# Plain blocks on TensorE, row sums in a column, one exp per head, and a new end: a change to a decode attention kernel that streams K and V

## The chip, the cores and the metric

The kernel runs on one core of a Trainium2 chip. The metric is the device time of one execution in microseconds (us). A ratio is the mean time of one kernel's fast runs over the mean of the other's fast runs of the same rounds, so it isn't quite the ratio of the medians that are quoted beside it.

## The reference

One query token attends to 65,536 keys. There are 32 query heads and 8 key heads, so 4 query heads share a key head, and the head dimension D is 128. Everything is bfloat16.

```python
B, Hq, Hkv, Sq, Sk, D = 1, 32, 8, 1, 65536, 128
scores = jnp.einsum("bhqd,bhkd->bhqk", q, k) * D ** -0.5
p = jax.nn.softmax(scores, axis=-1)
return jnp.einsum("bhqk,bhkd->bhqd", p, v)
```

K and V are 134.2 MB each. Every byte is used once.

## The kernel before

For each key head (G = 8) the K rows come in two loads of 8.39 MB (128 partitions x 256 slots x 128 elements), and so do the V rows. K has two buffers, V has one that is refilled in place. VectorE transposes K, TensorE computes scores, VectorE finds the maximum, ScalarE takes exp, VectorE transposes the weights, and TensorE multiplies them with V one head later. SyncE issues all loads, each as soon as the buffer is free:

```python
def load_k(g, b):
    SP.wait((s_sc, 16 * g - 8 + 8 * b if g else 0))     # scores of the head before are done
    ...
def load_v(g, b):
    done = 2 * (2 * g + b)
    if (g, b) == (G - 1, 1):                            # the last one comes in pieces
        ...
        for lo, hi, s in list(zip(CUTS, CUTS[1:], s_v))[1:]:
            load(v, g, b, 0, s, lo, hi)
    ...
    else:
        SP.wait((s_vc, done))                           # the V before has been multiplied
        load(v, g, b, 0, s_v[0])
        for s in s_v[1:4]:
            sp.sem_inc(s, 16)                           # credits for semaphores this load doesn't use
```

The softmax and TensorE's loop, cut:

```python
for b in range(4):
    a = act.activation(out=ex[:, b, :], in_=sc[:, 512 * b:512 * b + 512], func=ACT.Exp,
                       bias=nmb[:, :], scale=SCALE, accum_out=ls[:, b:b + 1])
...
with nc.Fori(0, G + 1, 1, engines=OrderedEngineSet([PE])) as h:
    ...
    gather(start=True, stop=True).then_inc(s_pe, 1)              # sums of the head before
    pe.matmul(out=pl, lhsT=sel[:, :], rhs=ls[:, :], ...)         # row sums of the head before
    with pe.Fori(0, 2) as j:
        with pe.If(h < G):
            with pe.Fori(0, 8) as n: ...                         # 8 score matmuls each
        with pe.If(h * 2 + j > 1):
            for ch in range(4):
                ...                                              # 16 matmuls with V each
                if ch == 1:
                    for _ in range(3):                           # fillers, result not used
                        pe.matmul(out=pt[0:16, :], lhsT=et[:, 0, 0:16], rhs=et[:, 0, :], ...)
```

After the loop come 24 small matmuls (128x4 by 128x128) for the last 24 slots of V, one at a time as the last pieces land, then a gather that adds up what was accumulated before, then the scale by 1/sum and the store:

```python
for x in range(TAIL):                                            # TAIL = 24
    if x % 8 == 0:
        pe.wait_ge(s_v[4 + x // 8], 16)
    pe.matmul(out=fin, lhsT=et[:, 1, w0:w0 + H], rhs=io[:, t, :], ...)
pe.wait_ge(s_vs, 1)
gather(start=False, stop=True).then_inc(s_pe, 1)
```

## Time and profile before

| | before |
|---|---|
| median of 3 runs | 631.59 us (631.14 to 631.75) |
| span of the profiled run | 629.3 us |
| bytes on the load queue | 268.44 MB |
| busy: TensorE, VectorE, ScalarE | 57%, 55%, 6% |
| one 8.39 MB load to the next, in the middle | 19.35 us, so 433.5 GB/s |
| last byte has landed | 625.32 us |

The first view is the page of the kernel before: busy time of each engine, then rows by slice (40 equal slices of the span, tenths; PEclk is TensorE's granted clock), then the DMA queues with packets, MB and share, and the exps of ScalarE with busy time and mean ns of one.

```profile
PE 355.6 (57%) x2176; PEld 141.5 (22%) x2176; DVE 347.1 (55%) x239; ACT 36.7 (6%) x72; POOL 7.4 (1%) x39
...
PEclk9999695976959789597896968869698696999568
DMA  8999999999999999999999999999999999999996
...
q1 hardware_dynamic: 6488, 268.44, 98.9%
...
q14 instruction: 4, 0.03, 0.0%
q8 instruction: 1, 0.02, 0.0%
...
L262 ACT ACTIVATE ex<-sc,nmb 128x512 bf16<-128x512 f32 x32 | 21.6, 686 | 556.1 <-DVE nmb L259 556.1
...
L262 ACT ACTIVATION_READ_ACCUMULATOR ex<-sc,nmb 128x1 f32 x32 | 6.5, 203 | 0.0
```

The DMA row is the one that is full, and the load queue keeps the DMA engines busy for 98.9% of the span. TensorE is idle for 43% of the span. Five small transfers on two queues are of the kind "instruction". I take them for fetches of code: with 128 more waits in VectorE's stream (dvewaits, below) three were recorded, at 13.8, 260.4 and 571.3 us, in place of the changed kernel's two.

The timeline of SyncE's queue in the middle shows when loads are issued (start us, us, what):

```profile
93.86 0.33 SPq L125 DMA_DIRECT2D io<-in_v_dram  x1
...
131.97 0.33 SPq L125 DMA_DIRECT2D io<-in_v_dram  x1
```

The landing of the transfer ahead of these V loads, from the records of landings: 101.67 us for the one issued at 93.86, and 140.38 us for the one issued at 131.97. In the middle a V load is always queued 8 to 9 us before the load ahead of it has landed on all 16 DMA engines. That is the slack of everything that computes.

The chain of waits, in order of time (start us, us, what; cut), shows the end:

```profile
610.52 13.57 DMA io<-in_v_dram
624.10 0.57 issue
624.66 1.50 PE pf L431 x24
626.16 0.23 PE pf L355 x2
...
```

A load is waited for, and then come small matmuls, gather, scale, store and the closing of the program: 4.0 us from the last landing (625.32) to the end of the span (629.30) in which no load moves.

### The profile page before, as it was taken

The numbers are of one execution on the slowest core, as the hardware profiler recorded it, in microseconds if no ns is written. First come the engines' busy times: TensorE is split into PE (matmuls) and PEld (weight loads), VectorE is DVE, ScalarE is ACT, GpSimd is POOL, SyncE is SP. The second block draws the span as 40 slices with busy tenths as digits, with TensorE's granted clock in tenths as the row PEclk, the third lists the DMA queues.
The fourth block names the chain that finished last, engine by engine and source line by source line (L and its number), as shares of the span: only waits on it lengthen the run. The fifth ranks groups of instructions, "written<-read, shape, count | busy, mean of one in ns | idle before, by whom it ended". The sixth has DMA issues, their size and how long they took to land. (4 is left out here: it accounts for less than half of the span.)

```text
span 629.3 us, 7142 instructions
## 1 busy us (share of the span) xinstructions
PE 355.6 (57%) x2176; PEld 141.5 (22%) x2176; DVE 347.1 (55%) x239; ACT 36.7 (6%) x72; POOL 7.4 (1%) x39
## 2 busy tenths in 40 slices
PE   0676581747627366382754728547184571886445
PEld 0222230312203122131321303213031230332112
DVE  4984925739066490665807557084670947684201
ACT  0000200020000200002000020000200002000100
POOL 1000000000000000000000000000000000000000
PEclk9999695976959789597896968869698696999568
DMA  8999999999999999999999999999999999999996
GB/s 367 433 459 408 458 408 455 412 454 412 454 412 454 417 450 417 450 417 450 421 446 421 446 425 442 425 442 425 446 425 442 429 437 429 409 433 431 431 428 247
DMA packets 6597, 268.50 MB, mean 427 GB/s; under 512 B 832, under 2 KB 832, under 8 KB 1344
## 3 DMA queue, kind: packets, MB, share of 16 engines
q1 hardware_dynamic: 6488, 268.44, 98.9%
q10 hardware_dynamic: 104, 0.02, 0.0%
q14 instruction: 4, 0.03, 0.0%
q8 instruction: 1, 0.02, 0.0%
HBM read 268.44 MB, written 0.01 MB: 427 GB/s over the span
## 5 line engine op out<-in xcount | busy, mean ns | idle before, releaser
L383 PE MATMUL sc<-io,wz 128*128 x1024 | 267.3, 411 | 201.5 <-PEq L345 158.4
L237 DVE STREAM_TRANSPOSE io<-io 128x4096 uint32<-128x4096 uint32 x64 | 279.8, 4417 | 162.8 <-DMA io<-in_k_dram 162.8
L383 PEld LDWEIGHTS sc<-io,wz 128*128 x1024 | 104.7, 102 | 361.0 <-issue 282.0
L359 PE MATMUL vacc<-io,et 128*16 128x512 bf16 x1018 | 73.5, 409 | 19.8 <-PEq L345 19.7
L262 ACT ACTIVATE ex<-sc,nmb 128x512 bf16<-128x512 f32 x32 | 21.6, 686 | 556.1 <-DVE nmb L259 556.1
L242 DVE TENSOR_REDUCE mx<-sc 128x1 f32<-128x512 f32 x32 | 20.8, 667 | 46.0 <-PE sc L383 46.0
L359 PEld LDWEIGHTS vacc<-io,et 128*16 128x16 bf16 x1018 | 27.7, 92 | 57.9 <-issue 35.8
L281 DVE STREAM_TRANSPOSE et<-ex 128x512 bf16<-128x512 bf16 x32 | 20.6, 683 | 15.4 <-PE vacc L359 13.5
L355 PE MATMUL pf<-vs,sel 128*4 128x128 f32 x20 | 5.4, 368 | 26.8 <-PEq L345 26.8
L251 DVE TENSOR_REDUCE m<-pt 1x4 f32<-1x128 f32 x8 | 2.2, 278 | 32.2 <-PE pt L419 32.2
L408 PE MATMUL pt<-et 128*16 128x512 bf16 x48 | 13.7, 397 | 0.0
L272 ACT ACTIVATE sc<-zero 128x2048 f32<-128x2048 f32 x7 | 13.2, 1880 | 0.3
L224 POOL COPY wz<-qT 32x16 bf16<-32x16 bf16 x32 | 6.1, 191 | 507.8 <-PE sc L383 502.5
L372 PE MATMUL pb<-ls,sel 128*4 128x4 f32 x18 | 1.8, 168 | 15.3 <-PEq L345 15.3
L290 DVE TENSOR_SCALAR vs<-vacc,sely 128x128 f32<-128x128 f32 x8 | 2.6, 324 | 13.3 <-PE vacc L359 13.3
L293 DVE SCALAR_TENSOR_TENSOR vs<-vacc,sely,vs 128x128 f32<-128x128 f32 x24 | 8.4, 351 | 0.8
L355 PEld LDWEIGHTS pf<-vs,sel 128*4 128x4 f32 x20 | 1.2, 83 | 27.2 <-issue 27.2
L262 ACT ACTIVATION_READ_ACCUMULATOR ex<-sc,nmb 128x1 f32 x32 | 6.5, 203 | 0.0
L421 PE MATMUL pb<-one,nrow 1*128 1x1 f32 x16 | 3.0, 254 | 5.7 <-PEq L345 5.7
L408 PEld LDWEIGHTS pt<-et 128*16 128x16 bf16 x48 | 4.6, 95 | 6.6 <-issue 1.6
L372 PEld LDWEIGHTS pb<-ls,sel 128*4 128x4 f32 x18 | 1.2, 88 | 18.9 <-issue 18.8
L421 PEld LDWEIGHTS pb<-one,nrow 1*128 1x128 f32 x16 | 2.5, 198 | 7.1 <-issue 7.1
(29 smaller groups left out, 25.5 us busy)
## 6 DMA issues: line engine op xcount, KB each, us to landing
io<-in_v_dram SPq DMA_DIRECT2D x5, 4096.0 KB, 15.7
io<-in_k_dram SPq DMA_DIRECT2D x4, 4096.0 KB, 26.0
io<-in_k_dram SPq DMA_DIRECT2D x4, 2048.0 KB, 38.8
io<-in_v_dram SPq DMA_DIRECT2D x1, 2048.0 KB, 11.1
io<-in_v_dram SPq DMA_DIRECT2D x1, 1024.0 KB, 13.3
io<-in_v_dram SPq DMA_DIRECT2D x4, 256.0 KB, 13.6
io<-in_k_dram SPq DMA_DIRECT2D x13, 46.6
io<-in_v_dram SPq DMA_DIRECT2D x13, 28.2
```

What stands on the lines that cost most here:

```text
L224: gp.tensor_copy(out=wz[r, :, c0:c0 + H].rearrange("p (s w) h -> p s w h", s=2), in_=qTb[r, :, :, g, :],).then_inc(s_w, 1)
L237: dve.transpose(out=part.bitcast(u32), in_=part.bitcast(u32)).then_inc(s_kt, 2)
L242: return DV.mark(dve.tensor_reduce(out=mx[:, b:b + 1], in_=sc[:, 512 * b:512 * b + 512], axis=AX.X, op=ALU.max))
L262: a = act.activation(out=ex[:, b, :], in_=sc[:, 512 * b:512 * b + 512], func=ACT.Exp, bias=nmb[:, :], scale=SCALE, accum_out=ls[:, b:b + 1],)
L272: ACTQ.mark(act.activation(out=sc[:, :], in_=zero[:, 0:1].to_broadcast([P, 4 * 512]), func=ACT.Copy))
L281: dve.transpose(out=et[:, i, :], in_=ex[:, 2 * b + i, :]).then_inc(s_et, 1)
L293: i = dve.scalar_tensor_tensor(out=vs[:, :], in0=vacc[:, y, :], scalar=sely[:, y:y + 1], in1=vs[:, :], op0=ALU.mult, op1=ALU.add,)
L355: return pe.matmul(out=fin, lhsT=sel[:, :], rhs=vs[:, :], skip_group_check=True, **kw)
L359: return pe.matmul(out=vacc[32 * c:32 * c + 16, :, :], lhsT=et[:, ch // 2, w0:w0 + 16], rhs=io[:, PS * ch + 4 * tt:PS * ch + 4 * tt + 4, : ...
L383: i = pe.matmul(out=bass.AP(sc, r_o, [[2048, P], [1, 512]]), lhsT=bass.AP(wz, r_w + ((2 * s + e) * WB - 4 * u), [[4 * WB, P], [1, P]]), rh ...
L408: pe.matmul(out=pt[0:16, :], lhsT=et[:, 0, 0:16], rhs=et[:, 0, :], start=True, stop=True,)
L421: pe.matmul(out=pb[:, 0:1], lhsT=nrow[:, :, :].rearrange("o x h -> o (x h)"), rhs=one[:, :], start=True, stop=True,).then_inc(s_pe, 1)
```

## The change

The intent: less work for TensorE's sequencer (one flat loop of plain blocks instead of nested loops with conditions), fewer instructions on ScalarE and VectorE, and a shorter end. The core of the diff, cut:

```diff
-CUTS = [0, 128, 192, 224, 232, 240, 248, 256]
+CUTS = [0, 128, 192, 224, 232, 240, 248, 252, 256]
...
-        for b in range(4):
-            a = act.activation(out=ex[:, b, :], in_=sc[:, 512 * b:512 * b + 512], ..., accum_out=ls[:, b:b + 1])
+        n = ACTQ.mark(act.activation(out=ex[:, :, :]..., in_=sc[:, :], ..., accum_out=ls[:, g % 2:g % 2 + 1]))
...
+            DV.mark(dve.tensor_copy(out=vs[:, D:D + 1], in_=ls[:, g % 2:g % 2 + 1]))
...
-            for s in s_v[1:4]:
-                sp.sem_inc(s, 16)
+            sp.sem_inc(s_v[1], 16)
...
-    finish(G - 1, 4 * G + 3, d_rl)
-    SP.wait((s_st, 16 * G))
+    n = ACTQ.mark(act.activation(out=o[:, :], in_=fin, func=ACT.Copy, scale=rl[:, :]))
+    ACTQ.after(n)
+    act.dma_start(out=out[0, (G - 1) * H:G * H, 0, :], in_=o[:, :]).then_inc(s_st, 16)
+    ACTQ.wait((s_st, 16 * G))
...
-    with nc.Fori(0, G + 1, 1, engines=OrderedEngineSet([PE])) as h:
-        ... nested Fori and If
+    with block("pe_head"):
+        take(s_w, 4)
+        gather(D + 1, start=True, stop=True).then_inc(s_pe, 1)
+        nc.br("pe_tile", engines=only)
+    ... blocks pe_tile, pe_part, pe_skip, pe_values, pe_rest, pe_next, pe_softmax, pe_tail
-                        for _ in range(3):
+                for _ in range(2):
```

So the last V piece is halved (4 slots, not 8), there are two fillers instead of three, and the last scale, store and final wait move from VectorE and SyncE to ScalarE.

More of the change, by code (lines that the diff above doesn't have):

```diff
@@ L88 @@
     nmb = sb("nmb", [P, 1], fp32)
-    ls = sb("ls", [P, 4], fp32)
-    l4 = sb("l4", [H, 1], fp32)
+    ls = sb("ls", [P, 2], fp32)
     rl = sb("rl", [H, 1], fp32)
@@ L93 @@
     et = sb("et", [P, 2, 512], bf16)
-    vs = sb("vs", [P, D], fp32)
+    vs = sb("vs", [P, D + 1], fp32)
     o = sb("o", [H, D], bf16)
@@ L101 @@
     pf = ps("pf", [P, 512])
-    pl, fin = pb[0:H, 8:12], pf[0:H, 0:D]
+    pl, fin = pb[0:H, 8:9], pf[0:H, 0:D]
     s_q, s_st = sem("s_q"), sem("s_st")
@@ L106, with down @@
     s_dv, s_ac, s_gp = sem("s_dv"), sem("s_ac"), sem("s_gp")
-    s_w, s_kt, s_mg, s_nr, s_ls, s_et, s_vs = (
-        sem("s_w"), sem("s_kt"), sem("s_mg"), sem("s_nr"), sem("s_ls"), sem("s_et"), sem("s_vs")
-    )
+    s_w, s_kt, s_mg, s_nr, s_et = sem("s_w"), sem("s_kt"), sem("s_mg"), sem("s_nr"), sem("s_et")
     s_sc, s_pe, s_vb, s_vc = sem("s_sc"), sem("s_pe"), sem("s_vb"), sem("s_vc")
+    def down(eng, which, s, n, wait=False):
+        w = dict(sync_type="semaphore", id=s.num, ant_name=s.name)
+        eng.add_instruction(mybir.InstEventSemaphore(
+            name=nc.get_next_instruction_name(), engine=which, sync_info=mybir.SyncInfo(
+                on_wait=[mybir.SyncWait(wait_mode="sem-ge-imm", wait_value=n, **w)] if wait else [],
+                on_update=[mybir.SyncUpdate(update_mode="sem-sub-imm", update_value=n, **w)],
+            ),
+        ))
     sp, act, dve, gp, pe = nc.sync, nc.scalar, nc.vector, nc.gpsimd, nc.tensor
@@ L153, in load_v @@
                 load(v, g, b, 0, s_v[i], 128 * i, 128 * i + 128)
-            for s in s_v[2:4]:
-                sp.sem_inc(s, 16)
         else:
@@ L158, in load_v @@
             load(v, g, b, 0, s_v[0])
-            for s in s_v[1:4]:
-                sp.sem_inc(s, 16)
+            sp.sem_inc(s_v[1], 16)
     load_k(0, 0)
     load_k(0, 1)
+    for s in s_v[2:4]:
+        sp.sem_inc(s, 16)
     for g in range(1, G):
@@ L181 @@
     DV.mark(dve.memset(one[:, :], 1.0))
-    n = DV.mark(dve.memset(ls[:, :], 0.0))
     d_zero = DV.mark(dve.memset(zero[:, :], 0.0))
@@ L187 @@
     n = DV.mark(dve.memset(vacc[:, :, :], 0.0))
-    DV.after(n)
-    dve.sem_inc(s_ls, 1)
-    dve.sem_inc(s_vs, 2)
+    collected = {-2: n, -1: n}
     DV.wait((s_gp, p_ident))
@@ L214 @@
     )
-    for g in range(G):
-        if g == 0:
-            GP.wait((s_dv, d_qT))
-            GP.after(p_ident)
-        else:
-            GP.wait((s_sc, 16 * g))
-        for a in range(4):
-            r = slice(32 * a, 32 * a + 32)
-            c0 = 28 + 32 * a
-            gp.tensor_copy(
-                out=wz[r, :, c0:c0 + H].rearrange("p (s w) h -> p s w h", s=2),
-                in_=qTb[r, :, :, g, :],
-            ).then_inc(s_w, 1)
-    GP.wait((s_sc, 16 * G))
-    gp.sem_inc(s_w, 4)
     def transposes(g, b):
@@ L249, in softmax @@
     def softmax(g):
-        DV.wait((s_pe, 4 * g + 3))
+        DV.wait((s_pe, 3 * g + 2))
         n = DV.mark(dve.tensor_reduce(
@@ L257, in softmax @@
         ).then_inc(s_nr, 1)
-        DV.wait((s_pe, 4 * g + 4))
+        DV.wait((s_pe, 3 * g + 3))
         d_nmb = DV.mark(dve.tensor_copy(out=nmb[:, :], in_=pb[:, 0:1]))
         ACTQ.wait((s_dv, d_nmb))
-        for b in range(4):
-            a = act.activation(
-                out=ex[:, b, :], in_=sc[:, 512 * b:512 * b + 512], func=ACT.Exp, bias=nmb[:, :],
-                scale=SCALE, accum_out=ls[:, b:b + 1],
-            )
-            ACTQ.mark(a)
-        n = ACTQ.n
+        n = ACTQ.mark(act.activation(
+            out=ex[:, :, :].rearrange("p b n -> p (b n)"), in_=sc[:, :], func=ACT.Exp,
+            bias=nmb[:, :], scale=SCALE, accum_out=ls[:, g % 2:g % 2 + 1],
+        ))
         if g == 0:
@@ L271, in softmax @@
             ACTQ.after(n)
-            ACTQ.mark(act.activation(
+            cleared[g] = ACTQ.mark(act.activation(
                 out=sc[:, :], in_=zero[:, 0:1].to_broadcast([P, 4 * 512]), func=ACT.Copy
             ))
-        act.wait_ge(s_ac, ACTQ.n)
-        act.sem_inc(s_ls, 1)
+    cleared = {}
     def weights(g, b):
         for i in range(2):
-            DV.wait((s_ac, 5 * g + 2 * b + i + 1))
+            DV.wait((s_ac, 2 * g + 1))
             dve.transpose(out=et[:, i, :], in_=ex[:, 2 * b + i, :]).then_inc(s_et, 1)
-    def reciprocal(g):
-        DV.wait((s_pe, 4 * g + 6))
-        n = DV.mark(dve.tensor_reduce(out=l4[:, :], in_=pl, axis=AX.X, op=ALU.add))
-        DV.after(n)
-        return DV.mark(dve.reciprocal(out=rl[:, :], in_=l4[:, :]))
@@ L289, in collect, with reciprocal @@
-    def collect(last=False):
-        n = DV.mark(dve.tensor_scalar_mul(out=vs[:, :], in0=vacc[:, 0, :], scalar1=sely[:, 0:1]))
+    def reciprocal(src, n_pe):
+        DV.wait((s_pe, n_pe))
+        return DV.mark(dve.reciprocal(out=rl[:, :], in_=src))
+    def collect(g):
+        n = DV.mark(dve.tensor_scalar_mul(out=vs[:, 0:D], in0=vacc[:, 0, :], scalar1=sely[:, 0:1]))
+        if g < G - 1:
+            DV.mark(dve.tensor_copy(out=vs[:, D:D + 1], in_=ls[:, g % 2:g % 2 + 1]))
         for y in range(1, 4):
@@ L292, in collect @@
             DV.after(n)
-            i = dve.scalar_tensor_tensor(
-                out=vs[:, :], in0=vacc[:, y, :], scalar=sely[:, y:y + 1], in1=vs[:, :],
+            n = DV.mark(dve.scalar_tensor_tensor(
+                out=vs[:, 0:D], in0=vacc[:, y, :], scalar=sely[:, y:y + 1], in1=vs[:, 0:D],
                 op0=ALU.mult, op1=ALU.add,
-            )
-            n = DV.mark(i)
-        if not last:
+            ))
+        if g < G - 1:
             DV.after(n)
             n = DV.mark(dve.memset(vacc[:, :, :], 0.0))
-        DV.after(n)
@@ L302, in collect, with finish @@
-        dve.sem_inc(s_vs, 1)
-    def finish(g, n_pe, d_rl):
-        DV.wait((s_st, 16 * g), (s_pe, n_pe))
+        collected[g] = n
+    def finish(g):
+        d_rl = reciprocal(pf[0:H, D:D + 1], 3 * g + 7)
+        DV.wait((s_st, 16 * g))
         DV.after(d_rl)
         n = DV.mark(dve.tensor_scalar_mul(out=o[:, :], in0=fin, scalar1=rl[:, :]))
-        Q = SP if g == G - 1 else ACTQ
-        Q.wait((s_dv, n))
-        Q.eng.dma_start(out=out[0, g * H:(g + 1) * H, 0, :], in_=o[:, :]).then_inc(s_st, 16)
+        ACTQ.wait((s_dv, n))
+        act.dma_start(out=out[0, g * H:(g + 1) * H, 0, :], in_=o[:, :]).then_inc(s_st, 16)
@@ L326, with gather @@
         if g:
-            d_rl = reciprocal(g - 1)
             DV.wait((s_vc, 4 * g))
-            collect()
+            collect(g - 1)
         weights(g, 0)
         if g:
-            finish(g - 1, 4 * g + 5, d_rl)
+            finish(g - 1)
     DV.wait((s_vc, 4 * G - 2))
+    for s in s_v[2:4]:
+        down(dve, mybir.EngineType.DVE, s, 16)
     weights(G - 1, 1)
-    d_rl = reciprocal(G - 1)
     DV.wait((s_vb, 2 * G))
-    collect(last=True)
-    finish(G - 1, 4 * G + 3, d_rl)
-    SP.wait((s_st, 16 * G))
-    def take(s, n):
-        w = dict(sync_type="semaphore", id=s.num, ant_name=s.name)
-        pe.add_instruction(mybir.InstEventSemaphore(
-            name=nc.get_next_instruction_name(), engine=PE, sync_info=mybir.SyncInfo(
-                on_wait=[mybir.SyncWait(wait_mode="sem-ge-imm", wait_value=n, **w)],
-                on_update=[mybir.SyncUpdate(update_mode="sem-sub-imm", update_value=n, **w)],
-            ),
-        ))
+    collect(G - 1)
+    d_rl = reciprocal(pl, 3 * G + 2)
+    ACTQ.wait((s_st, 16 * (G - 1)), (s_dv, d_rl), (s_pe, 3 * G + 3))
+    n = ACTQ.mark(act.activation(out=o[:, :], in_=fin, func=ACT.Copy, scale=rl[:, :]))
+    ACTQ.after(n)
+    act.dma_start(out=out[0, (G - 1) * H:G * H, 0, :], in_=o[:, :]).then_inc(s_st, 16)
+    ACTQ.wait((s_st, 16 * G))
+    for g in range(G):
+        if g == 0:
+            GP.wait((s_dv, d_qT))
+            GP.after(p_ident)
+        else:
+            GP.wait((s_sc, 16 * g))
+        for a in range(4):
+            r = slice(32 * a, 32 * a + 32)
+            c0 = 28 + 32 * a
+            if a == 3:
+                GP.wait((s_dv, collected[g - 2]), (s_ac, cleared.get(g - 1, 0)))
+            gp.tensor_copy(
+                out=wz[r, :, c0:c0 + H].rearrange("p (s w) h -> p s w h", s=2),
+                in_=qTb[r, :, :, g, :],
+            ).then_inc(s_w, 1)
+    GP.wait((s_sc, 16 * G), (s_dv, collected[G - 2]))
+    gp.sem_inc(s_w, 4)
+    def take(s, n):
+        down(pe, PE, s, n, wait=True)
     IO = 3 * SL * D
-    def gather(**kw):
-        return pe.matmul(out=fin, lhsT=sel[:, :], rhs=vs[:, :], skip_group_check=True, **kw)
+    def gather(w, **kw):
+        return pe.matmul(
+            out=pf[0:H, 0:w], lhsT=sel[:, :], rhs=vs[:, 0:w], skip_group_check=True, **kw
+        )
     def wide(ch, tt):
@@ L364, in wide @@
         )
-    with nc.Fori(0, G + 1, 1, engines=OrderedEngineSet([PE])) as h:
-        take(s_w, 4)
-        take(s_vs, 1)
-        gather(start=True, stop=True).then_inc(s_pe, 1)
-        take(s_ls, 1)
-        pe.matmul(out=pl, lhsT=sel[:, :], rhs=ls[:, :], start=True, stop=True).then_inc(s_pe, 1)
-        with pe.Fori(0, 2) as j:
-            with pe.If(h < G):
-                with pe.Fori(0, 8) as n:
-                    r_k = j * (SL * D) + (n // 2) * (PS * D) + (n % 2) * (2 * D) + SL * D
-                    r_w = (n % 4) * (-8) + 28
-                    r_o = j * 1024 + (n // 4) * 512
-                    take(s_kt, 1)
-                    for u in range(2):
-                        for s in range(2):
-                            for e in range(2):
-                                i = pe.matmul(
-                                    out=bass.AP(sc, r_o, [[2048, P], [1, 512]]),
-                                    lhsT=bass.AP(
-                                        wz, r_w + ((2 * s + e) * WB - 4 * u), [[4 * WB, P], [1, P]]
-                                    ),
-                                    rhs=bass.AP(
-                                        io, r_k + (u * D + 64 * s + e),
-                                        [[IO, P], [4 * D, 16], [2, 32]],
-                                    ),
-                                    start=False, stop=False, skip_group_check=True,
-                                )
-                    i.then_inc(s_sc, 1)
-            with pe.If(h * 2 + j > 1):
-                take(s_et, 2)
-                for ch in range(4):
-                    if ch != 1:
-                        take(s_v[max(ch - 1, 0)], 16)
-                    for tt in range(16 if ch < 3 else (SL - TAIL) % PS // 4):
-                        if (ch, tt) == (3, 8):
-                            take(s_v[3], 16)
-                        i = wide(ch, tt)
-                    if ch == 1:
-                        i.then_inc(s_vc, 1)
-                        for _ in range(3):
-                            pe.matmul(
-                                out=pt[0:16, :], lhsT=et[:, 0, 0:16], rhs=et[:, 0, :],
-                                start=True, stop=True,
-                            )
-                i.then_inc(s_vb, 1)
-                with pe.If(h * 2 + j < 2 * G + 1):
-                    for tt in range((SL - TAIL) % PS // 4, 16):
-                        i = wide(3, tt)
-                    i.then_inc(s_vc, 1)
-        with pe.If(h < G):
-            take(s_mg, 1)
-            pe.transpose(out=pt[0:1, 0:P], in_=mg[:, :], identity=ident[:, :]).then_inc(s_pe, 1)
-            take(s_nr, 1)
@@ new lines, with block @@
+    only = OrderedEngineSet([PE])
+    r_x, r_n = (nc.alloc_registers(r, engines=only) for r in ("x", "n"))
+    def block(name):
+        return nc.body(name, valid_engines=only)
+    nc.regs_mov(r_x, -1)
+    nc.br("pe_head", engines=only)
+    with block("pe_head"):
+        take(s_w, 4)
+        gather(D + 1, start=True, stop=True).then_inc(s_pe, 1)
+        nc.br("pe_tile", engines=only)
+    with block("pe_tile"):
+        nc.regs_alu(r_x, r_x, 1, op=ALU.add)
+        nc.regs_mov(r_n, -1)
+        nc.br_cmp(r_x, 2 * G, "pe_part", "pe_skip", "IS_LT", engines=only)
@@ new lines @@
+    with block("pe_part"):
+        nc.regs_alu(r_n, r_n, 1, op=ALU.add)
+        x = nc.snap(r_x, engines=only, donate=True, min_val=0, max_val=2 * G + 1)
+        n = nc.snap(r_n, engines=only, donate=True, min_val=0, max_val=7)
+        r_k = (x % 2) * (SL * D) + (n // 2) * (PS * D) + (n % 2) * (2 * D) + SL * D
+        r_w = (n % 4) * (-8) + 28
+        r_o = (x % 2) * 1024 + (n // 4) * 512
+        take(s_kt, 1)
+        for u in range(2):
+            for s in range(2):
+                for e in range(2):
+                    i = pe.matmul(
+                        out=bass.AP(sc, r_o, [[2048, P], [1, 512]]),
+                        lhsT=bass.AP(wz, r_w + ((2 * s + e) * WB - 4 * u), [[4 * WB, P], [1, P]]),
+                        rhs=bass.AP(
+                            io, r_k + (u * D + 64 * s + e), [[IO, P], [4 * D, 16], [2, 32]]
+                        ),
+                        start=False, stop=False, skip_group_check=True,
+                    )
+        i.then_inc(s_sc, 1)
+        nc.br_cmp(r_n, 7, "pe_part", "pe_skip", "IS_LT", engines=only)
@@ new lines @@
+    with block("pe_skip"):
+        nc.br_cmp(r_x, 2, "pe_next", "pe_values", "IS_LT", engines=only)
+    with block("pe_values"):
+        take(s_et, 2)
+        for ch in range(4):
+            if ch == 3:
+                pe.wait_ge(s_v[2], 16)
+            elif ch != 1:
+                take(s_v[ch // 2], 16)
+            for tt in range(16 if ch < 3 else (SL - TAIL) % PS // 4):
+                if (ch, tt) == (3, 8):
+                    pe.wait_ge(s_v[3], 16)
+                i = wide(ch, tt)
+            if ch == 1:
+                i.then_inc(s_vc, 1)
+                for _ in range(2):
+                    pe.matmul(
+                        out=pt[0:16, :], lhsT=et[:, 0, 0:16], rhs=et[:, 0, :],
+                        start=True, stop=True,
+                    )
+        i.then_inc(s_vb, 1)
+        nc.br_cmp(r_x, 2 * G + 1, "pe_rest", "pe_tail", "IS_LT", engines=only)
@@ new lines @@
+    with block("pe_rest"):
+        for tt in range((SL - TAIL) % PS // 4, 16):
+            i = wide(3, tt)
+        i.then_inc(s_vc, 1)
+        nc.br("pe_next", engines=only)
+    with block("pe_next"):
+        nc.regs_alu(r_n, r_x, 2, op=ALU.mod)
+        nc.br_cmp(r_n, 0, "pe_tile", "pe_softmax", "IS_EQ", engines=only)
+    with block("pe_softmax"):
+        take(s_mg, 1)
+        pe.transpose(out=pt[0:1, 0:P], in_=mg[:, :], identity=ident[:, :]).then_inc(s_pe, 1)
+        take(s_nr, 1)
+        pe.transpose(
+            out=pb[:, 0:1], in_=nrow[:, :, :].rearrange("o x h -> o (x h)"), identity=one[:, :]
+        ).then_inc(s_pe, 1)
+        nc.br("pe_head", engines=only)
@@ L421 @@
+    nc.switch_bb("pe_tail")
+    for t in range(SL - TAIL, SL):
+        if t == CUTS[5]:
             pe.matmul(
-                out=pb[:, 0:1], lhsT=nrow[:, :, :].rearrange("o x h -> o (x h)"), rhs=one[:, :],
-                start=True, stop=True,
+                out=pl, lhsT=sel[:, :], rhs=ls[:, (G - 1) % 2:(G - 1) % 2 + 1], start=True, stop=True
             ).then_inc(s_pe, 1)
-    for x in range(TAIL):
-        t = SL - TAIL + x
-        if x % 8 == 0:
-            pe.wait_ge(s_v[4 + x // 8], 16)
-        w0 = t % PS // 4 * 32 + 16 + 4 * (x % 4)
+        if t in CUTS:
+            pe.wait_ge(s_v[CUTS.index(t)], 16)
+        w0 = t % PS // 4 * 32 + 16 + 4 * (t % 4)
@@ L431 @@
         pe.matmul(
-            out=fin, lhsT=et[:, 1, w0:w0 + H], rhs=io[:, t, :], start=(x == 0), stop=False,
+            out=fin, lhsT=et[:, 1, w0:w0 + H], rhs=io[:, t, :], start=(t == SL - TAIL), stop=False,
             skip_group_check=True,
         )
-    pe.wait_ge(s_vs, 1)
-    gather(start=False, stop=True).then_inc(s_pe, 1)
+    pe.wait_ge(s_dv, collected[G - 1])
+    gather(D, start=False, stop=True).then_inc(s_pe, 1)
 _INS = ['q', 'k', 'v']
```

## The prediction

> **What bounds it.** The stream of K and V from HBM. The queue table gives 268.44 MB on the load queue; the activity by slice shows the DMA engines at nine tenths or more from the second slice to the last but one. In the packets, all 16 engines have work from 2.0 us to about 622 us. One 8.39 MB load lands every 19.35 us, so 433.5 GB/s[...]. 32 x 19.35 = 619.2 us. The rest is fixed: 2.0 us before the first byte; some 2 us at the end in which the engines finish unevenly; 4.0 us from the last landing (625.3) to the end of the span (629.3).
>
> TensorE (57% busy), VectorE (55%) and ScalarE (6%) are off this path. SyncE issues the middle V loads 8 to 9 us before the transfer ahead of them has landed (issued 131.97, previous landing 140.38), so the rings never run dry.
>
> **What the change removes, adds, moves.**
> - Plain blocks, fewer register operations, two instead of three filler matmuls: perhaps 1 us of TensorE a head, off the critical path.
> - One exp of 128x2048 for four of 128x512. Four cost 4 x (686 + 203) = 3.56 us; from 686 ns for 512 columns and 1880 ns for 2048 (the clearing copy) I estimate 2.1 us. Hidden under the 8 us of slack.
> - Row sums as a column of vs: a 4-column matmul (168 ns a pass) and a reduction (about 110 ns) go, a one-column copy comes, eight times. Hidden.
> - Fewer SyncE credits (17 ns each): hidden.
> - Last V piece halved: after the last landing 4 small matmuls remain instead of 8, at 62 ns (24 took 1.50 us), so 0.25 us off the critical path. Its 1 KB packets may give back 0.05 us.
> - Last scale on ScalarE: I estimate 0.39 us (0.29 fixed plus 128 x 0.78 ns) against 0.34 us on VectorE; store issue 0.26 us (median of its earlier stores) against 0.35 us on SyncE. With the hops, net about -0.1 us.
>
> **The uncertain term.** The 16 landings of one load come within 0.45 us of each other early on; at the end the slowest trails the first by 2.3 us, while 11 are within 0.5 us. The lag grows in steps, after instruction fetches at 41.6 us (16 KB), 106.9, 375.4, 417.5 and 561.6 (8 KB each). Because the rings never empty, an engine that fetched never catches up. [...] The new streams are a little shorter, so a fetch may go, or fall on another engine: I put -0.2 us with a spread of 0.9.
>
> **Sum.** 631.6 - 0.25 - 0.1 - 0.2 + 0.05 = 631.1 us, range 629.8 to 632.0. Faster by over 2%: 0.5%; within 2%: 99%; slower: 0.5%.
>
> **What would show it.** Right: DMA nine tenths everywhere, a load every 19.35 us, more TensorE idle time rather than a shorter span; the chain of waits ending in the last V load, four small matmuls, gather, ScalarE, store; the last landing within 1 us of 625.3. Wrong step: a gap in the DMA row in the middle (a V load issued late because the exp comes as one piece), a very different fetch count, or more than 4.0 us from last landing to end of span.
>
> **What would make it wrong.** A stall of the load queue; TensorE fetching code in every pass, which would lag DMA engines; a faster transfer rate, of which I see no sign.

The sum came to 631.1 us, and all its terms stand. The two marked cuts are statements that no trace or run here shows; the one on fetches stood behind the thought that a shorter stream may lose a fetch, so that the -0.2 us is a guess of mine. The 0.39 us for the scale are an estimate from the same two durations as the 2.1 us for the exp: the line through 686 ns at 512 columns and 1880 ns at 2048 rises by 0.78 ns a column and starts at 0.29 us. The 0.05 us for 1 KB packets were a guess too; in the traces a 2,048-byte packet takes 84 ns (before) and a 1,024-byte one 46 ns (after), so 16 of these on a DMA engine in place of 8 cost 0.06 us.

## The result, and the profile after

| | before | after |
|---|---|---|
| median of 6 runs, same rounds | 631.37 us (630.98 to 632.65) | 631.54 us (630.51 to 631.78) |
| ratio | | 0.9997, 95% interval 0.9984 to 1.0010 |
| span of the profiled run | 629.30 us | 629.39 us |
| instructions in the trace | 7142 | 6741 |
| code fetches from 2 us to the last landing | 5 | 2 |
| last byte has landed | 625.32 us | 625.33 us |
| from there to the end of the span | 3.98 us | 4.06 us |

The time is the same. The page of the changed kernel, the lines that answer to those above:

```profile
PE 350.6 (56%) x2136; PEld 138.0 (22%) x2136; DVE 346.9 (55%) x236; ACT 31.3 (5%) x25; POOL 7.4 (1%) x39
...
PEclk9999595977959779697896968869698696999577
DMA  8999999999999999999999999999999999999996
...
q1 hardware_dynamic: 6624, 268.44, 98.9%
...
q8 instruction: 1, 0.02, 0.0%
q14 instruction: 2, 0.02, 0.0%
...
L249 ACT ACTIVATE ex<-sc,nmb 128x2048 bf16<-128x2048 f32 x8 | 15.8, 1969 | 560.9 <-DVE nmb L247 560.9
```

TensorE is busy 5.0 us less, ScalarE 5.4 us (36.7 before, 31.3 after), and the DMA row hasn't changed. The exp of a head went from 4 x (686 + 203) ns to one of 1969 ns and its read of the sum. None of it shows in the span. SyncE's queue at the same place as before:

```profile
94.66 0.33 SPq L132 DMA_DIRECT2D io<-in_v_dram  x1
...
130.81 0.33 SPq L132 DMA_DIRECT2D io<-in_v_dram  x1
```

The loads are issued at the same times within 1.2 us, still 6 to 9 us before the load ahead of them has landed (100.57 and 139.68). The end of the chain of waits, though, looks different from what I had expected:

```profile
609.60 13.11 DMA io<-in_v_dram
...
622.76 1.45 PE vacc L360 x8
624.21 0.87 PE pf L454 x8
...
625.11 1.38 PE pf L454 x16
626.48 0.23 PE pf L354 x2
...
626.82 0.36 ACT o L323
```

The last 16 small matmuls take 1.38 us of the chain, where I had counted on 62 ns each. The timelines of the end side by side, first of the kernel before, then of the changed one:

```profile
624.66 1.50 PE L431 MATMUL pf<-io,et 128*4 128x128 bf16 x24 [0.65 <-DMA io<-in_v_dram]
...
626.00 0.38 PE L355 MATMUL pf<-vs,sel 128*4 128x128 f32 x2
626.48 0.34 DVE L307 TENSOR_SCALAR o<-pf,rl 4x128 bf16<-4x128 f32 x1 [0.91 <-PE pf L355]
626.84 0.35 SPq L310 DMA_DIRECT2D out_dram<-o  x1
```

```profile
624.06 1.01 PE L454 MATMUL pf<-io,et 128*4 128x128 bf16 x8
...
624.97 1.51 PE L454 MATMUL pf<-io,et 128*4 128x128 bf16 x16
...
626.32 0.38 PE L354 MATMUL pf<-vs,sel 128*4 128x128 f32 x2
626.82 0.36 ACT L323 ACTIVATE o<-pf,rl 4x128 bf16<-4x128 f32 x1 [33.39 <-PE pf L354]
627.21 0.26 ACTq L325 DMA_DIRECT2D out_dram<-o  x1
```

Before, 24 small matmuls take 1.50 us. After, TensorE starts 0.6 us earlier: in the kernel before, the trace has four branches and two register operations of TensorE's sequencer between 623.67 and 624.61 us, and in the changed kernel one branch, at 623.44, before the matmuls with V have ended. But it is done 0.3 us later: single starts lie 106 to 107 ns apart instead of 56. In both runs 12 of the 24 start after the last landing (counted in the traces), not the 8 and the 4 that I had predicted: before, because TensorE comes late to them, and after, because it is slow. The stretches of the end say why (header of the view first; the third to last column, PEclk, is the granted clock, 1.00 is full speed). Before:

```profile
core 0: us, PE busy (x) PEld busy (x) DVE busy (x) ACT busy (x) POOL busy (x), PEclk, DMA share, GB/s
...
619.00:622.50 3.50, 1.80 (x23) 0.45 (x18) 0.00 (x0) 0.00 (x0) 0.00 (x0) 1.00 1.00 390
622.50:625.00 2.50, 1.33 (x17) 0.60 (x18) 0.87 (x3) 0.00 (x0) 0.00 (x0) 1.00 0.29 110
625.00:626.00 1.00, 1.00 (x22) 1.00 (x19) 0.53 (x2) 0.00 (x0) 0.00 (x0) 1.00 0.00 0
```

After:

```profile
619.00:622.50 3.50, 1.63 (x22) 0.35 (x16) 0.00 (x0) 0.00 (x0) 0.00 (x0) 0.98 1.00 389
622.50:625.00 2.50, 2.24 (x21) 1.14 (x22) 0.70 (x2) 0.00 (x0) 0.00 (x0) 0.51 0.37 125
625.00:626.00 1.00, 1.00 (x14) 1.00 (x13) 0.76 (x3) 0.00 (x0) 0.00 (x0) 0.51 0.06 16
```

In the changed kernel's run TensorE's clock was at one half from 622.6 to 626.0 us, where TensorE is the critical engine. In the run of the kernel before it stayed full.

### The profile page after: what moved, and what is told of

Read it like the earlier page. It is cut to its first block, busy times and chain, and to the rows that moved or that the text cites. A ratio compares the mean times of both kernels' runs of the same rounds, so it can differ in the third digit from the quotient of the medians.

```text
span 629.4 us, 6741 instructions
## 1 busy us (share of the span) xinstructions
PE 350.6 (56%) x2136; PEld 138.0 (22%) x2136; DVE 346.9 (55%) x236; ACT 31.3 (5%) x25; POOL 7.4 (1%) x39
## 5 line engine op out<-in xcount | busy, mean ns | idle before, releaser
L360 PE MATMUL vacc<-io,et 128*16 128x512 bf16 x1018 | 70.9, 411 | 21.6 <-PEq L114 20.2
L249 ACT ACTIVATE ex<-sc,nmb 128x2048 bf16<-128x2048 f32 x8 | 15.8, 1969 | 560.9 <-DVE nmb L247 560.9
L354 PE MATMUL pf<-vs,sel 128*4 128x129 f32 (+1 forms) x20 | 5.7, 386 | 42.0 <-PEq L114 42.0
L422 PE MATMUL pt<-et 128*16 128x512 bf16 x32 | 9.7, 384 | 0.0
L440 PE MATMUL pb<-one,nrow 1*128 1x1 f32 x8 | 1.6, 196 | 5.7 <-PEq L114 5.7
L284 DVE MEMSET vacc<- 128x512 f32 x7 | 3.4, 485 | 1.3 <-DVE vs L278 1.3
L422 PEld LDWEIGHTS pt<-et 128*16 128x16 bf16 x32 | 3.0, 93 | 4.1 <-issue 0.6
L247 DVE COPY nmb<-pb 128x1 f32<-128x1 f32 x8 | 1.3, 159 | 3.0 <-PE pb L440 3.0
L438 PE MATMUL pt<-ident,mg 128*1 128x128 f32 x8 | 2.3, 282 | 1.1 <-PEq L114 1.1
```

The lines of the kernel that those rows point to most:

```text
L249: n = ACTQ.mark(act.activation(out=ex[:, :, :].rearrange("p b n -> p (b n)"), in_=sc[:, :], func=ACT.Exp, bias=nmb[:, :], scale=SCALE, acc ...
L284: n = DV.mark(dve.memset(vacc[:, :, :], 0.0))
L354: return pe.matmul(out=pf[0:H, 0:w], lhsT=sel[:, :], rhs=vs[:, 0:w], skip_group_check=True, **kw)
L360: return pe.matmul(out=vacc[32 * c:32 * c + 16, :, :], lhsT=et[:, ch // 2, w0:w0 + 16], rhs=io[:, PS * ch + 4 * tt:PS * ch + 4 * tt + 4, : ...
```

## The experiments

Two questions were open. Why does the end not get shorter (theory A: TensorE's clock; rival B: accident; rival C: TensorE's work in the middle matters)? And why does the last landing not move though three fetches of code before it are gone (theory D: VectorE's fetches all delay one DMA engine, which ends last; rival E: fetches don't matter)? Of these three, two are no longer recorded, and the one of 16 KB is recorded at 625.4 us, just after that landing. "The base" in the texts is the run called warm.

### Three fillers again

```diff
-                for _ in range(2):
+                for _ in range(3):
```

> The changed kernel with three filler matmuls after the second chunk of V, as before the change, instead of two. Theory A (the shorter tail was given back because TensorE's granted clock fell to one half from 622.6 to 626.0 us[...]): the clock stays at full speed there, the last small matmuls start 56 ns apart instead of 107, and the gather ends at about 626.2 us instead of 626.7; time 0.3 to 0.5 us less than the changed kernel's. Rival B (the clock's phase in the tail is an accident of the run): the clock may be either, and the time is unchanged within 0.4 us.

Measured: 630.73, 630.75, 630.93, 631.96 and 631.96 us (ratio to before 0.9990, 0.9976 to 1.0003). The profiled run is one of the two longer ones, and its stretches are:

```profile
622.50:625.00 2.50, 1.65 (x21) 0.76 (x22) 0.81 (x3) 0.00 (x0) 0.00 (x0) 1.00 0.40 137
625.00:626.00 1.00, 1.00 (x12) 1.00 (x13) 0.66 (x3) 0.00 (x0) 0.00 (x0) 0.61 0.08 19
626.00:627.00 1.00, 1.00 (x9) 0.57 (x6) 0.00 (x0) 0.00 (x0) 0.00 (x0) 0.50 0.00 0
```

The clock fell to one half again, only later, at 625.2 us. From the last landing to the gather's end it took 1.49 us, no less than with two fillers (1.37). So that half of theory A falls: with three fillers in the usual place the clock fell as well. But the runs come in two groups some 1.0 us apart, as one expects if the clock is sometimes full and sometimes half in the last 3 us (only the profiled run's clock is known that finely). Rival B is right about one run, in that the phase varies, and what the phase costs is what theory A says.

### Fillers in the gap before the end

```diff
+            if ch == 2:
+                for _ in range(3):
+                    pe.matmul(out=pt[0:16, :], lhsT=et[:, 0, 0:16], rhs=et[:, 0, :], start=True, stop=True)
```

> The changed kernel with three more fillers after the third chunk of V, so in the gap that the tail waits in for the fourth. Theory A: full clock from 619 us to the end, small matmuls 56 ns apart, gather ends 0.9 us or less after the last landing instead of 1.37 us, time 0.4 us less than the changed kernel's. If TensorE is off the critical path elsewhere, the extra 16 x 3 x 0.2 to 0.4 us of matmuls cost nothing and a load still lands every 19.35 us. Rival C (TensorE work in the middle matters): time longer by some us.

Measured: 630.61 to 631.27 us, median 630.73 (ratio 0.9986, 0.9973 to 1.0000). The stretches, and the timeline of the end:

```profile
619.00:622.50 3.50, 1.73 (x20) 0.62 (x19) 0.00 (x0) 0.00 (x0) 0.00 (x0) 1.00 1.00 399
622.50:625.00 2.50, 1.99 (x27) 1.11 (x28) 1.07 (x4) 0.00 (x0) 0.00 (x0) 1.00 0.39 137
625.00:626.00 1.00, 0.89 (x15) 0.59 (x11) 0.40 (x2) 0.00 (x0) 0.00 (x0) 1.00 0.00 0
```

```profile
624.01 0.61 PE L460 MATMUL pf<-io,et 128*4 128x128 bf16 x8 [0.23 <-DMA io<-in_v_dram]
...
624.62 1.05 PE L460 MATMUL pf<-io,et 128*4 128x128 bf16 x16
...
625.51 0.38 PE L354 MATMUL pf<-vs,sel 128*4 128x128 f32 x2
626.01 0.36 ACT L323 ACTIVATE o<-pf,rl 4x128 bf16<-4x128 f32 x1 [31.58 <-PE pf L354]
626.40 0.26 ACTq L325 DMA_DIRECT2D out_dram<-o  x1
```

The clock is full to the end, the 24 small matmuls run at 56 ns, and from the last landing (625.23) to the gather's end it takes 0.66 us instead of 1.37. The fillers made TensorE 11.3 us busier than the changed kernel (361.9 against 350.6 us) and the kernel got no slower. That refutes rival C.

> The version with fillers after the third chunk again, as the base of the next runs and to see whether its narrow spread repeats: 630.6 to 631.3 us, small matmuls 56 ns apart, gather ends 0.7 us after the last landing. If its first five runs were luck (rival B), some runs now lie above 631.5 us as they do for the changed kernel.

The repeat, on another occasion: 630.67 to 631.12 us, median 631.00 (ratio 0.9983, 0.9969 to 0.9996). All ten runs of this version lie between 630.61 and 631.27 us. The changed kernel's six, of other rounds, lie between 630.51 and 631.78, and four of them above 631.3. The clock itself is recorded for the profiled runs alone: in all nine of versions with these fillers it is full from the last V pieces to the store, and in three of the five without them (after, fill3, b_tail, but not before and dvewaits) it falls to one half. The cleanest pair needs no filler: dvewaits, told below, has the TensorE code of the changed kernel and happened to be at full clock, and from its last landing to the gather's end it took 0.66 us against 1.37. I take theory A's cost as shown.

### The kernel before, with the same fillers

The same three lines in the old loop, in addition to its three fillers.

> The kernel before with three more fillers after the third chunk of V. Theory A (the clock of the tail, not the change, decides whether a run takes 631 or 632 us): its runs no longer spread to 632.8 us, all are within 0.7 us, small matmuls 56 ns apart, gather ends about 1.0 to 1.1 us after the last landing, because TensorE leaves its loop late and has 24 small matmuls before it; median 631.0 us, 0.3 us above the changed kernel with the same fillers. If the time does not change or the spread stays (rival B), the clock is not what spreads the runs.

Measured: 631.00 to 631.53 us, median 631.31 (ratio 0.9987, 0.9974 to 1.0001), while the unaltered kernel before spread from 631.03 to 632.96 in the same rounds. From last landing to gather's end 1.00 us. That fits a kernel before that also loses time to its clock in some runs, though its one trace shows full clock. With the clock held, the changed kernel is ahead by 0.31 us (631.31 against 631.00, same rounds, five runs each whose ranges just overlap). I take that as the gain of the change once it isn't covered up.

### The new end alone, on the kernel before

`CUTS` with 252, a wait at each cut, scale and store and final wait on ScalarE; nothing else.

> The kernel before with the new tail only: last V piece halved, last scale and store on ScalarE. My prediction's sum: 0.3 us faster than before. Theory A: three fillers are there, so the tail runs at full clock, but TensorE still leaves its loop at about 624.6 us and then works through a backlog of 24 small matmuls, so the gather ends at most 0.1 us earlier than in the kernel before (626.4 us); time within 0.2 us of before.

Measured: 631.71 to 632.81 us, median 632.06 (ratio 1.0003, 0.9989 to 1.0016). I expected full clock because three fillers are there, and missed: the 24 small matmuls ran at half clock, with starts from 625.19 to 627.59, and the gather ended 2.37 us after the last landing. TensorE left its loop at 625.1 us, though the V piece that its first small matmuls need had landed at 624.65, which supports the point that leaving the nested loop late costs; but the miss is of the same kind as in the first experiment. How many fillers are in the usual place doesn't by itself decide the clock. So the comparison that this run was made for, the new end in the old loop at full clock, was not had.

### Undoing one part of the end at a time, with the clock held

Last piece of 8 slots again (`CUTS` without 252), on top of the version with fillers:

> The version with fillers, its last V piece again 8 slots instead of 4. With the clock at full speed in the tail, my prediction's step holds: from the last landing to the gather's end 0.88 us instead of 0.67, so 0.2 us; time 0.2 us above the base. Rival: VectorE's sums (ready some 0.1 us after the last landing) hide the difference and it is under 0.1 us.

Measured: 631.04 to 631.34 us, median 631.16 (ratio 0.9991, 0.9979 to 1.0003). From the last landing to the gather's end 0.87 us against 0.66 and 0.68, and 8 small matmuls start after the last landing against 4: the halved piece is worth 0.2 us, and the rival falls.

Last scale on VectorE, last store and wait on SyncE again:

> The version with fillers, its last scale on VectorE and its last store and wait on SyncE, as before the change. I predicted 0.1 us in favour of ScalarE. The traces so far say: from the gather's end to the landing of the store 1.66 us on ScalarE and 1.65 on VectorE and SyncE, but from that landing to the end of the span 1.03 us against 1.27. So 0.2 us longer than the base, all of it after the landing.

Measured: five runs from 630.80 to 631.19 and one of 633.14 us, median 631.00 (ratio 0.9995, 0.9979 to 1.0010). The time doesn't resolve it. The trace does: from the store's landing to the end of the span 1.27 us, against 1.03 with ScalarE. The trace also shows what lies there. When SyncE has the last wait, it then signals the other engines, which drain and signal back, and it takes their answers; when ScalarE has it, the others have done their part before the store lands, and ScalarE's answer alone is missing. From the end of the wait to SyncE's last step of this it takes 0.5 us in the one and 0.25 us in the other; what follows is the same.

The end of every run of this kind and of dvewaits, worked out from the traces (us; the last column is the sum of the three before it, to rounding):

| run | last landing | to gather's end | to store landed | to end of span | after last landing |
|---|---|---|---|---|---|
| before | 625.32 | 1.06 | 1.65 | 1.27 | 3.98 |
| before + fillers (b_warm) | 625.79 | 1.00 | 1.65 | 1.27 | 3.93 |
| before + new end (b_tail), half clock | 625.97 | 2.37 | 1.66 | 1.03 | 5.06 |
| after, half clock | 625.33 | 1.37 | 1.66 | 1.03 | 4.06 |
| after, 3 fillers (fill3), half clock | 625.59 | 1.49 | 1.65 | 1.03 | 4.16 |
| after + 128 waits (dvewaits), full clock by chance | 626.44 | 0.66 | 1.65 | 1.03 | 3.33 |
| after + fillers (warm) | 625.23 | 0.66 | 1.66 | 1.03 | 3.34 |
| the same again (warm2) | 625.55 | 0.68 | 1.66 | 1.03 | 3.36 |
| warm, last piece of 8 slots | 625.33 | 0.87 | 1.67 | 1.03 | 3.56 |
| warm, end on VectorE and SyncE | 625.20 | 0.66 | 1.65 | 1.27 | 3.58 |

With the clock held, the change shortens the end by 0.6 us (3.93 to 3.34): 0.2 us by the halved piece, 0.25 us by the engine that holds the last wait, and the rest, a little over 0.1 us, I put down to TensorE reaching its small matmuls earlier: with a last piece of 8 slots and full clock 11 of them start after the last landing in the old loop (b_warm) and 8 in the new one, 1.00 against 0.87 us. These two differ in the rest of the change too, so no run isolates it. With the clock at half, 0.7 us go back.

### Adding to what delays the last DMA engine

```diff
     DV.wait((s_q, 16))
+    for _ in range(128):
+        DV.wait((s_gp, p_ident))
```

In the changed kernel the two fetches come after 49 and 175 of VectorE's recorded instructions, so 126 apart; from that, and by estimate, 128 more waits bring one fetch more.

> The changed kernel with 128 more semaphore waits that are already satisfied on VectorE at its start[...]. Theory D (VectorE's fetches, recorded at 106.8 and 415.1 us, delay one and the same DMA engine by about 0.95 us each, and that engine ends last): three such fetches, the slowest engine's lag over the first at the end 2.7 us instead of 1.7, last landing about 626.3 us, time 0.9 us longer than the changed kernel's. Rival E (fetches fall on any engine, or an engine makes up for them): last landing within 0.3 us of 625.3 and no change of time.

Measured: fetches at 13.8, 260.4 and 571.3 us instead of 106.8 and 415.1, as they must be if VectorE's stream is what is fetched. Last landing 626.44 us, 1.1 later. The lags in the landings read as one engine hit each time: the lag of the last engine over the first was 1.1 us before the second fetch, 2.1 after it and 3.1 after the third, while the last but one stayed at 0.9 (before the tail: 0.91 and 1.11 at 235 us, 0.90 and 2.07 at 293, 0.88 and 3.08 at 575). But the time was 631.43 to 632.52, median 631.54 (ratio 1.0000, 0.9987 to 1.0014), as of the changed kernel: in the profiled run the clock was full in the end, with 3.33 us after the last landing. Inconclusive as to time, so again with the clock held:

> That version with the 128 satisfied waits on VectorE at its start. The first try of these waits moved the last landing by 1.1 us but its time was blurred by the clock of the tail, which is now fixed. Theory D (VectorE's fetches add up on one DMA engine, and that engine's end is the kernel's end): last landing 626.3 us, time 0.9 to 1.1 us above the base, 631.7 us. Rival E (the lag is absorbed): time as the base within 0.3 us.

Measured: 632.06 to 633.25 us, median 632.55, against 631.00 of the base in the same rounds (ratio to before 1.0010, 0.9996 to 1.0024). Last landing 626.54 us against 625.55. One more fetch of VectorE's code costs 1.0 us of landing and at least that of time (the two profiled runs are 632.06 and 631.02 us, 1.0 apart; why the medians are 1.5 apart is open. One 16 KB fetch fell at 525.3 us in this run, on an engine that wasn't the last one). Rival E falls.

### Taking a fetch away

A VectorE stream of some 180 instead of 280 instructions: K transposes of 128 slots instead of 64, weights and maxima joined, collecting of heads 0 to 6 left out. The output is wrong.

```diff
-        for t0 in range(0, SL, PS):
+        step = PS if (g, b) == (G - 1, 1) else 2 * PS
+        for t0 in range(0, SL, step):
...
+        if g < G - 1:            # in collect
+            collected[g] = DV.n
+            return
```

> That version with a VectorE stream of some 170 instead of 280 instructions: two transposes or reductions joined in one, and the collecting of heads 0 to 6 left out, so the output of these heads is wrong on purpose. Theory D: its second fetch (recorded at about 415 us) is gone, the slowest DMA engine trails the first by 0.8 us instead of 1.7, last landing 624.4 to 624.6 us, time 0.6 to 0.9 us below the base, 629.9 us. Rival E: one fetch less but the last landing stays near 625.3 us and the time is the base's within 0.3 us.

Measured: 644.03 to 645.76 us, median 645.17 (ratio 1.0207, 1.0191 to 1.0222). A miss that teaches: the second fetch is gone, but SyncE's queue says

```profile
104.48 0.33 SPq L132 DMA_DIRECT2D io<-in_v_dram  x1
```

against a landing of the load ahead at 103.51 us. The V load is issued some 9 us later than in warm (95.28). I put that down to scores beginning later when a K transpose covers 128 slots; the next run, which joins other steps but not these, isn't starved. TensorE frees the V buffer later, the load is issued after the queue has run empty, and 14 us are lost over the eight heads. The slack of 8 us is real, and it is finite.

So the same without joining the K transposes; instead one maximum over all scores, the scaling of heads 0 to 6 left out, and the copy of the bias on ScalarE (171 VectorE instructions, wrong):

> The version with fillers, and a VectorE stream of some 170 instead of 280 instructions, this time without joining the K transposes (that starved the load queue): joined transposes of the weights and maxima, collecting and scaling of heads 0 to 6 left out (their outputs wrong on purpose), the bias copy on ScalarE. Theory D: only one VectorE fetch is left, the slowest DMA engine trails the first by about 0.8 to 1.2 us instead of 1.7 to 2.2, last landing 624.4 to 624.8 us, time 630.0 to 630.4 us against 630.7 to 631.0 of the base. Rival E: last landing near 625.3 us all the same, time the base's.

Measured: five runs from 629.87 to 630.32 and one of 631.45 us, median 630.13 (ratio 0.9977, 0.9964 to 0.9991). The time came out as theory D expects. The landing did not: 625.03 us, and the slowest DMA engine still trailed the first by 1.7 us, because a 16 KB fetch at 368.3 us had hit another engine. That other engine then ends last, but by 0.1 us only: the one that the fetch at 184.9 us hit ends next, at 624.91, and it trailed the first by 1.6 us as well, because it was 0.66 us late before that fetch, without a recorded one. So the removal is half a confirmation: last landing earlier by only 0.2 to 0.5 us, median below those of the base by 0.6 to 0.9. The base was not run in these rounds; by the ratios to the kernel before (0.9977 against 0.9986 and 0.9983) it is 0.4 to 0.6 us, and the intervals overlap. What else makes up the difference in time is open, as these are different executions.

### Bytes

240 of 256 slots for one V load in the middle, all work left in (wrong):

```diff
-            load(v, g, b, 0, s_v[0])
+            load(v, g, b, 0, s_v[0], 0, 240 if (g, b) == (2, 0) else SL)
```

> The version with fillers, with 240 instead of 256 slots of one V load in the middle (wrong on purpose: stale rows are used for the rest); 0.52 MB less of 268.44, all the work is left in. If bytes over 433.5 GB/s bound the kernel: 1.2 us less than the base. If something else paces it (rival: the TensorE or VectorE loop), no change.

Measured: 629.41 to 630.11 us, median 629.58 (ratio 0.9967, 0.9955 to 0.9979). That is 1.2 to 1.4 us below the medians of the base, which was run in other rounds, and 1.0 to 1.2 us by the ratios to the kernel before (0.9967 against 0.9983 and 0.9986), for 0.2% of the bytes. Bytes set the pace of the middle.

### The fetches in the traces

Worked out from the packet and landing records, not from a view: a 65,536-byte packet takes 2418 to 2422 ns in three cases of four, and in the kernel before 98% are under 2430 ns. The packets over 2750 ns there are at 42.7 us (2909), 107.2 (3080), 375.7 (2800) and 417.8 (3082), each just after a fetch of code (41.6, 106.9, 375.4, 417.5). After the fifth fetch (561.6) the packets are smaller, and one of 16,384 bytes took 1024 ns instead of 611 to 624. An 8 KB fetch itself takes 309 to 332 ns, and with the 660 ns by which the next packet is stretched that makes the 1 us of lag. In the changed kernel the slow ones are at 107.1 (3056) and 415.4 (3080), after its two fetches, and at 41.6 (3053), where no fetch is recorded. Most other runs too have slow packets near 41.5 us without one: either the records aren't complete, or something else than a fetch delays packets there. The landings of the last piece on the 16 DMA engines:

```text
           first    median   last but one   last
before    623.06    623.40        624.84   625.32
after     623.63    623.74        624.24   625.33
```

Before, several engines lag by different amounts; after, only one lags far, and it is as late as the last one was. In the kernel before, the engine that the fetch at 417.5 us hit trailed by 1.3 us and then by 2.24, and ended last; those of the fetches at 41.6, 375.4 and 561.6 us trailed by 1.8, 1.0 and 0.7 us. In the changed kernel the last one's lag grew by 1 us with the fetch at 415.1 us (landings of the load that ended next: last but one 429.91, last 431.00, before it 410.56 and 410.68). So the fetches that the change removed had hit engines that weren't last. Whose code they were, no run tells; two of them are still there in b_tail (375.9 and 562.3 us), so the new end isn't what removed them. That the other engines landed later in this run than before is not explained; it grew between 140 and 178 us, where packets took up to 2655 ns without a fetch, and it costs nothing as long as one engine is later still.

Not settled: which sequencer fetches the single 16 KB block. It came at 41.6 us before and at 625.4 us after, but at 525.3, 448.0 and 368.3 us in versions whose TensorE code is the same as in warm, where it came at 624.5.

## Why the prediction was right or wrong

The range held: 631.54 us in 629.8 to 632.0. The point, 631.1, was 0.4 us low. The time alone tests little: the forecast gain of 0.5 us lies inside the interval of the ratio (0.9984 to 1.0010, so -1.0 to +0.6 us), and the end took as long as before (4.06 against 3.98 us) because a gain and a half-rate clock cancelled. That the range held is in part luck. Two of the signs that the prediction itself gave for a wrong step came: more than 4.0 us from the last landing to the end of the span (4.06), and a very different fetch count. Three terms need correcting.

- **What bounds it: right.** The DMA row is unchanged, a load lands every 19.35 us, and the run with fewer bytes is faster by the time of those bytes. TensorE's and ScalarE's savings (5.0 and 5.4 us busy) went into idle time under a slack of 8 us.
- **The step that failed: "4 small matmuls remain instead of 8, at 62 ns", 0.25 us off.** The duration came from one run of the kernel before in which TensorE's clock was full. In the changed kernel's run it was half and matmuls came 107 ns apart, so landing to gather's end grew from 1.06 to 1.37 us. The counts were off too: 12 small matmuls, not 8, remained in the kernel before, since TensorE left its nested loop late, and 12, not 4, in the changed one, since it was slow. With the clock held full in the new loop it is 4 against 8, and the halved piece is worth 0.2 us (0.87 against 0.66): mechanism right, both conditions missed. What makes the clock rise and fall is not shown. The clock records of the changed kernel's end change in steps of 3.4 us (619.1, 622.6, 626.0), the runs of fill3 fall in two groups, and three of five profiled runs without the fillers in the gap were at half in the end. I had looked only at the durations.
- **"Last scale on ScalarE, net about -0.1 us": right in sign, in the wrong place.** Gather's end to store landed is unchanged (1.65 and 1.66). The 0.25 us is after the landing (1.27 to 1.03), because SyncE's exchange with the other engines at the close of the program comes after its own last wait, and mostly before that of ScalarE ends (0.5 us of it are left after the wait in the run before, 0.25 us in the changed kernel's).
- **The fetches, "-0.2 us with a spread of 0.9": the count fell more than thought, from five to two, and the last landing moved by 0.01 us.** The fetches that went weren't on the DMA engine that ends last. I had written that an engine that fetched never catches up, and in the traces it didn't (a lag of 1.85 us lasts from 61 to 411 us in the kernel before, one of 1.8 us from 431 to 620 us in the changed one); but only the slowest engine counts.
- **One exp in place of four, credits, row sums, blocks: hidden, right.** I had estimated 2.1 us for the exp; it takes 1.97 us and the read of the sum.

So the change does gain, about 0.3 us in time and 0.6 us in the end of the trace, with the clock held. In the plain comparison that is hidden in the spread of the runs, to which the clock of the last 3 us adds up to 0.7 us.

## What to carry to other kernels

In this kernel, bound by its loads, only the bytes, the first microseconds (2.0 us before the first byte) and the end count, and in the end an engine with idle time before it was the critical one at half clock (0.51 of full speed from 622.5 to 626.0 us of the changed kernel's trace). With three unused matmuls in TensorE's last waiting gap of each V load the clock was full at the end in all nine profiled runs, and the changed kernel with them is the best correct version here, medians of 630.7 and 631.0 us against 631.5 for the changed kernel and 631.4 to 632.1 for the one before (different rounds in part). When a saving leaves the time alone, ask which of 16 parallel engines ends last and whether the saving touched that one; and check that a shared queue keeps its slack before joining steps that free a buffer.
